# A two-layer attention and MLP kernel: row blocks transposed through DRAM in the opening, attention weights fetched from another queue

## The chip, the cores and the metric

The kernel runs on one core of a Trainium2 chip. The metric is the device time of one execution in microseconds (us), the median of the runs shown. Before the change it is 2496.91 us (three runs, 2496.49 to 2500.01).

A core has five engines that run side by side, each through its own list of instructions in order: TensorE (PE; its weight loads are PEld), VectorE (DVE), ScalarE (ACT), GpSimd (POOL) and SyncE (SP). ACT and SP also issue transfers (DMAs). An instruction that waits, for an engine or for a transfer to land, holds up all that stands behind it on its engine.

## The reference, cut to what matters

```python
def A(x, wqkv, w_phi, wo):               # S=2048, D=576, H=32, Dh=18
    q, k, v = split_heads(x @ wqkv)
    pq, pk = einsum("bhsd,hdf->bhsf", q, w_phi), einsum("bhsd,hdf->bhsf", k, w_phi)
    phi_q = concat([softmax(pq), softmax(-pq)])
    phi_k = concat([softmax(pk), softmax(-pk)])
    kv = einsum("bhsf,bhsd->bhfd", phi_k, v)
    z = einsum("bhsf->bhf", phi_k)
    num = einsum("bhqf,bhfd->bhqd", phi_q, kv)
    den = einsum("bhqf,bhf->bhq", phi_q, z)[..., None] + 1e-6
    return merge_heads(num / den) @ wo

def B(x, w1, b1, w2, b2):                # F=4608
    h = relu(x @ w1 + b1)
    return (h * h) @ w2 + b2

x = A_x
x = x + A(layernorm(x)); x = x + B(layernorm(x))
x = x + A(layernorm(x)); x = x + B(layernorm(x))
```

All is float32. There is no mask: the key totals `kv` and `z` need all 2048 rows before one query row can be finished.

## The kernel before, in words

**Precision.** A float32 operand of a matmul is kept as two parts, high and low: ACT writes the high part (rounded), DVE subtracts it from the original and gets the low part. A product is three matmuls, high x high, low x high and high x low.

**Tiling.** The 2048 rows are four blocks of 512 (`b` 0 to 3), a block four tiles of 128 rows (`t`). The opening numbers its 16 tiles straight through: `N` or `T` = 4b + t. The 576 columns are four chunks of 128 (`KC`) and a tail of 64 (`DT`). A matmul needs the normalized rows transposed, with columns on the partitions; the transposed block is a dict with `h` and `l`, the two parts.

**Stages.** The opening (0 to about 262 us) folds `w_phi` into the q and k weights, normalizes all 16 tiles, makes keys and values of every tile and adds them to the totals, and makes the queries of the last block in full, those of the others as raw rows parked in DRAM (`qs`). Behind it stands a barrier, where the totals are complete. Then come the four dense blocks of the first layer in the order 3, 2, 0, 1 (each 36 steps of 128 hidden columns, `m_3ph`, `m_2ph` and so on), with the attention of the next block and the second layer's keys and values of the previous block woven in between their steps; then a shorter second opening, `between` (1349 to 1475 us), and the four dense blocks of the second layer.

**The order of the work.** PE, ACT, DVE and POOL carry out their instructions in the order in which the program writes them. A `Plan` sets it: `plan.on(slot, depth, call, ...)` and `plan.put` put a call into a slot, and within a slot calls of a larger depth are written first (9 comes first; the projections of a slot have 0; -1 comes behind them). In the opening a slot is one half of a projection of one tile (14 matmuls). SP is not ordered by hand: a scheduler places its transfers, most of them well ahead of need.

**The line of the opening.** The list `line` gives each `T` the slots of its key projection (`k`), the value projection of the next tile (`v`) and, for `T` from 2 to 9, raw queries (`far`): six slots for each `T` in that stretch. Behind each key projection comes its soft part, on the path DVE (two maxima `s0K..m`, a difference `s0K..e`), POOL (the second difference), ACT (the exponential `s0K..e`), DVE (sums `s0K..r`, reciprocal, scaling), and later PE adds keys times values (`kvp`, `ks.add`). Also in the opening, `PrepareO` splits the output weights piece by piece into their parts (`oh` by ACT, `or` by DVE), one piece with each `T` from 4 to 8.

**Layer norm and transposes in the opening.** Class `Norm`: `stats` (DVE: BN_STATS twice, BN_AGGR; POOL: the reciprocal root), `scale_by_act` (ACT writes the normalized row, 512 columns into `n_..n` and 64 into `n_..e`), `turn` (PE transposes four 128x128 pieces into PSUM, `n_..p`; ACT writes the high part from there, DVE the low part) and `rest` (the same for the tails of two tiles at once, two transposes). All four blocks of the opening use it. In the profile its names have the block's number: `n_2n` belongs to block 2, so to the tiles `N` = 8 to 11.

**The way through DRAM.** Class `TripNorm` is there already and serves the dense blocks: the normalized row is written with its columns regrouped, stored to a scratch array in DRAM (`xrm`, the tails `xrt`) by a DMA that ACT issues, fetched back by another that ACT issues (`n`; on odd tiles also the tails of the pair, `e`), flipped in 32x32 pieces by one DVE instruction (STREAM_TRANSPOSE, `flip`), and split by ACT and DVE from SBUF. PE has no part in it. The fetch reads what the store wrote, so ACT waits at the fetch until the store has landed.

**Attention weights.** `asked(which, name)` makes tiles for one of the four weights and four calls that load it in pieces, as DMAs of SP. `plan_keys` asks for the second layer's `v` and `k` weights, once in each dense block but the first; the next block's attention asks for `o`. In the loop of `body` these calls have depth 9.

## Time and profile before

| | |
|---|---|
| median of three runs | 2496.91 us (2496.49 to 2500.01) |
| the profiled execution | 2497.19 us, its span 2495.5 us |
| PE busy | 2478.5 us, 99% of the span |
| DVE busy | 1260.1 us, 50% |
| ACT busy | 788.1 us, 32% |
| opening and barrier | 0 to 262 us |
| dense blocks of layer 0 | 262 to 1349 us |

A row of the timeline has the start in us, the duration, the engine, the line and operation, and what is written from what; in square brackets the idle time of the engine just before it and what ended that. Numbers of buffers are left out of names. `xN` counts instructions that were joined into one row. "ACTq" and "SPq" are the issue of a DMA by that engine; the transfer itself lasts beyond it. A row of the windows gives for a stretch its length, the busy time of each engine, the granted clock of PE, the share of time in which the 16 DMA engines were busy, and GB/s.

### The profile page before, as it was taken

Reading aid. Unit: us, or ns where it says so; the run is one execution under the profiler, and the core shown is the slowest. Engines: PE = TensorE matmul, PEld = TensorE weight load, DVE = VectorE, ACT = ScalarE, POOL = GpSimd, SP = SyncE. Lnnn points to the kernel's source line nnn. Section 1 sums busy time; section 2 is a strip of 40 time slices with the busy share of each in tenths; the row PEclk is TensorE's granted clock in tenths of the full one; section 3 lists DMA queues with packets and bytes.
Section 4 is the critical chain, followed back from the end, with each engine's and each line's share of the span. In section 5 each row is a group of like instructions: output and inputs, shape, how many; then the busy total and the mean of one; then the engine's idle time right before and its main releaser. Section 6 shows DMA issues by size and latency. Waiting matters only on the chain.

```text
span 2495.5 us, 37635 instructions
## 1 busy us (share of the span) xinstructions
PE 2478.5 (99%) x14968; PEld 2182.9 (87%) x14968; DVE 1260.1 (50%) x2214; ACT 788.1 (32%) x1439; POOL 189.4 (8%) x539
## 2 busy tenths in 40 slices
PE   9999999999999999999999999999999999999999
PEld 8999888888888888888888988888888888888887
DVE  6679885545744476455113776433453436442112
ACT  5444453422232223223213332413233222312212
POOL 4211100000200001000000011000110002000000
PEclk9999999999999999999999999999999999999999
DMA  9313698986767677684565248678576867676565
GB/s 321 98 54 92 243 315 266 310 315 205 259 229 271 217 206 273 216 298 146 195 199 182 92 141 263 209 217 291 186 257 204 261 219 246 217 230 230 194 199 171
DMA packets 214374, 545.07 MB, mean 218 GB/s; under 512 B 29006, under 2 KB 96814, under 8 KB 214198
## 3 DMA queue, kind: packets, MB, share of 16 engines
q1 hardware_dynamic: 163638, 500.44, 60.8%
q10 hardware_dynamic: 50560, 42.21, 5.3%
q8 instruction: 119, 1.95, 0.3%
q14 instruction: 57, 0.47, 0.1%
HBM read 439.20 MB, written 103.38 MB: 217 GB/s over the span
## 4 chain that ended last, share of the span: by engine, by line
PE 95%; DMA 2%; DVE 1%; ACT 1%; issue 1%; SPq 0%; ACTq 0%; DVEq 0%
PE m_1ph L975 9%; PE m_3ph L975 9%; PE m_0ph L975 9%; PE m_2ph L975 9%; PE m_1acc L1000 7%; PE m_3acc L1000 7%; PE m_2acc L1000 7%; PE m_0acc L1000 7%; PE m_1acc L992 2%; PE m_3acc L992 2%; PE m_2acc L992 2%; PE m_0acc L992 2%; PE a_0po L816 1%; PE a_2po L816 1%; PE kvp L593 1%; PE a_3po L816 1%
## 5 line engine op out<-in xcount | busy, mean ns | idle before, releaser
L975 PE MATMUL m_2ph<-a_2nh,m_2h 128*128 128x512 f32 x720 | 225.2, 394 | 1.2 <-ACT m_2hr L980 0.7
L975 PE MATMUL m_0ph<-a_0nh,m_0h 128*128 128x512 f32 x720 | 225.0, 394 | 1.3 <-ACT m_0hr L980 1.1
L1000 PE MATMUL m_3acc<-m_3s,m_3hb 128*128 128x448 f32 x864 | 189.3, 367 | 0.4 <-DVE m_3hb L984 0.4
L1000 PE MATMUL m_1acc<-m_1s,m_1hb 128*128 128x448 f32 x864 | 189.0, 367 | 0.3 <-PE m_1ph L975 0.3
L1000 PE MATMUL m_2acc<-m_2s,m_2hb 128*128 128x448 f32 x864 | 188.9, 367 | 0.0
L1000 PE MATMUL m_0acc<-m_0s,m_0hb 128*128 128x448 f32 x864 | 188.8, 367 | 0.0
L984 DVE CAST m_2hb<-m_2hr 128x512 fp32r<-128x512 f32 x72 | 31.2, 433 | 292.4 <-ACT m_2hr L981 292.3
L1000 PEld LDWEIGHTS m_1acc<-m_1s,m_1hb 128*128 128x128 f32 x864 | 161.9, 188 | 18.8 <-PE m_1ph L975 0.5
L1000 PEld LDWEIGHTS m_3acc<-m_3s,m_3hb 128*128 128x128 f32 x864 | 161.2, 188 | 17.8 <-PE m_3ph L975 0.6
L1000 PEld LDWEIGHTS m_2acc<-m_2s,m_2hb 128*128 128x128 f32 x864 | 161.6, 188 | 17.2
L1000 PEld LDWEIGHTS m_0acc<-m_0s,m_0hb 128*128 128x128 f32 x864 | 161.6, 188 | 17.2
L975 PEld LDWEIGHTS m_2ph<-a_2nh,m_2h 128*128 128x128 f32 x720 | 135.3, 188 | 32.7 <-ACT m_2hr L980 1.2
L975 PEld LDWEIGHTS m_0ph<-a_0nh,m_0h 128*128 128x128 f32 x720 | 135.2, 188 | 32.8 <-ACT m_0hr L980 1.5
L984 DVE CAST m_1hb<-m_1hr 128x512 fp32r<-128x512 f32 x72 | 30.7, 427 | 258.8 <-ACT m_1hr L981 258.8
L980 ACT ACTIVATE m_2hr<-m_2ph,b1t 128x512 f32<-128x512 f32 x72 | 49.6, 689 | 339.1 <-PE m_2ph L975 327.4
L980 ACT ACTIVATE m_1hr<-m_1ph,b1t 128x512 f32<-128x512 f32 x72 | 49.6, 689 | 319.1 <-PE m_1ph L975 309.1
L980 ACT ACTIVATE m_0hr<-m_0ph,b1t 128x512 f32<-128x512 f32 x72 | 49.6, 689 | 317.2 <-PE m_0ph L975 288.6
L984 DVE CAST m_0hb<-m_0hr 128x512 fp32r<-128x512 f32 x72 | 31.5, 438 | 229.0 <-ACT m_0hr L981 229.0
L984 DVE CAST m_3hb<-m_3hr 128x512 fp32r<-128x512 f32 x72 | 31.7, 440 | 173.6 <-ACT m_3hr L981 173.6
L980 ACT ACTIVATE m_3hr<-m_3ph,b1t 128x512 f32<-128x512 f32 x72 | 49.6, 689 | 219.3 <-PE m_3ph L975 209.2
L975 PE MATMUL m_3ph<-t0onh,m_3h 128*128 128x512 f32 (+1 forms) x380 | 112.9, 384 | 0.6 <-ACT t0onh L385 0.5
L975 PE MATMUL m_1ph<-t1onh,m_1h 128*128 128x512 f32 (+1 forms) x380 | 112.4, 382 | 0.8 <-ACT t1onh L385 0.5
(2050 smaller groups left out, 5734.9 us busy)
## 6 DMA issues: line engine op xcount, KB each, us to landing
m_2h<-dw SPq DMA_DIRECT2D x72, 640.0 KB
m_0h<-dw SPq DMA_DIRECT2D x72, 640.0 KB
...
```

What stands on the lines that cost most here:

```text
L593: nc.tensor.matmul(po[32 * q : 32 * q + 32, :, j], vt[:, h * VW : h * VW + 32], e[:, :, h * DH : (h + 1) * DH], start=not stay, stop=True, ...
L816: nc.tensor.matmul(pt[:, :HP], a, m[:w, g], start=(g == 0 and k == 0), stop=(g == NG - 1 and k == 2))
L975: nc.tensor.matmul(ph[:, cols], a, m, start=(k == 0), stop=(k == 3 * KC + 1))
L980: nc.scalar.activation(hr, ph, AF.Relu, bias=b1t[:, f : f + 1])
L984: nc.vector.tensor_copy(hh, hr)
L992: nc.tensor.matmul(acc[KC], a, m, start=(f == 0 and k == 0), stop=(f == NF - 1 and k == 2))
L1000: nc.tensor.matmul(acc[t][:, :R], a[:, rows], m, start=(f == 0 and k == 0), stop=(f == NF - 1 and k == 2))
```

## The change

It has two parts that do not touch one another.

In the opening, blocks 2 and 3 (tiles 8 to 15) get a `TripNorm` in place of a `Norm`: their transposes go through DRAM and DVE, tails included. `TripNorm` gets a `scale_by_act`, so that ACT and not DVE writes the row. Loads and `stats` of these tiles come one slot earlier than before, those of block 3 five slots earlier, and `scale` comes one to eight slots earlier; store, fetch and flip get slots of their own, each behind that slot's projections.

In the dense blocks of layer 0, the loads of the second layer's `v` and `k` weights and of the next blocks' `o` weights are issued by ACT, at depth -1, in place of SP at depth 9; the totals of the tiles 2 and 3 of each block are added one turn later.

```diff
--- before.py
+++ after.py
@@ -299,7 +299,7 @@
                 nc.sync.dma_start(d.rearrange("p (h c n) -> p h c n", h=2, c=NC)[:w, :, g],
                                   piece.rearrange("p (h n) -> p h n", h=2))
 
-    def asked(which, name, tags=TAGS_A):
+    def asked(which, name, tags=TAGS_A, by=nc.sync):
 
         pair, calls = [], []
 
@@ -307,7 +307,7 @@
             if k == 0:
                 pair.append(piece_tiles(f"{name}{which}{half}", tags))
             for d, piece in moved(which, half, k, pair[half][k]):
-                nc.sync.dma_start(piece, d)
+                by.dma_start(piece, d)
 
         return pair, [lambda half=half, k=k: ask(half, k) for half in range(2) for k in range(2)]
 
@@ -400,17 +400,31 @@
             super().__init__(dst, name, then)
             self.b, self.trips, self.tails, self.row = b, trips, tails, {}
 
+        def ends(self, h):
+            return self.xd.rearrange("p t e -> p (t e)")[h * DT : (h + 1) * DT]
+
+        def begin(self, t):
+            if not self.tails and self.xd is None:
+                self.xd = sb.tile([P, NT, DT], F32, tag="xd", name=f"{self.name}e", bufs=1)
+            row = self.row[t] = sb.tile([P, D], F32, tag="qk", name=f"{self.name}r{t}", bufs=5)
+            return [(row[:, : KC * P].rearrange("p (a b c) -> p b a c", a=KC, b=KC),
+                     slice(0, KC * P)), (row[:, KC * P :] if self.tails else self.xd[:, t], slice(KC * P, D))]
+
+        def scale_by_act(self, t):
+            if t not in self.trips:
+                return super().scale_by_act(t)
+            x, (nmr, rstd) = self.x.pop(t), self.stat.pop(t)
+            for dst, cols in self.begin(t):
+                src = x[:, cols] if cols.start else x[:, cols].rearrange("p (b a c) -> p b a c", a=KC, b=KC)
+                nc.scalar.activation(dst, src, AF.Identity, bias=nmr, scale=rstd)
+
         def scale(self, t):
             if t not in self.trips:
                 return super().scale(t)
             x, (mv, rstd) = self.x.pop(t), self.stat.pop(t)
-            if self.xd is None:
-                self.xd = sb.tile([P, NT, DT], F32, tag="xd", name=f"{self.name}e", bufs=1)
-            row = self.row[t] = sb.tile([P, D], F32, tag="qk", name=f"{self.name}r{t}", bufs=5)
-            args = dict(scalar1=mv[:, 0:1], scalar2=rstd, op0=ALU.subtract, op1=ALU.mult)
-            nc.vector.tensor_scalar(row[:, : KC * P].rearrange("p (a b c) -> p b a c", a=KC, b=KC),
-                                    x[:, : KC * P].rearrange("p (b a c) -> p b a c", a=KC, b=KC), **args)
-            nc.vector.tensor_scalar(row[:, KC * P :] if self.tails else self.xd[:, t], x[:, KC * P :], **args)
+            for dst, cols in self.begin(t):
+                src = x[:, cols] if cols.start else x[:, cols].rearrange("p (b a c) -> p b a c", a=KC, b=KC)
+                nc.vector.tensor_scalar(dst, src, scalar1=mv[:, 0:1], scalar2=rstd, op0=ALU.subtract, op1=ALU.mult)
             if self.then:
                 self.then(t, x)
 
@@ -422,13 +436,12 @@
                 nc.scalar.dma_start(xrt[self.b][t].rearrange("a p f -> p a f"),
                                     row[:, KC * P :].rearrange("p (a f) -> p a f", f=32))
 
-        def ends(self, h):
-            return self.xd.rearrange("p t e -> p (t e)")[h * DT : (h + 1) * DT]
-
         def fetch(self, t):
             xn = self.xn[t] = sb.tile([P, KC * P], F32, tag="xn", name=f"{self.name}n{t}")
             nc.scalar.dma_start(xn, xrm[self.b][t].rearrange("a (r g) f -> (a r) (g f)", g=KC))
             if self.tails and t % 2:
+                if self.xd is None:
+                    self.xd = sb.tile([P, NT, DT], F32, tag="xd", name=f"{self.name}e", bufs=1)
                 nc.scalar.dma_start(self.ends(t // 2).rearrange("p (t f) -> p t f", t=2),
                                     xrt[self.b][t - 1 : t + 1].rearrange("t a (r g) f -> (a r) t (g f)", g=KC))
 
@@ -1288,7 +1301,8 @@
         vpair = [piece_tiles(f"w0v{h}", TAGS_A) for h in range(2)]
         fold = Fold(kpair, vpair)
         xT = [{} for _ in range(NB)]
-        norms = [Norm(xT[b], f"n0_{b}") for b in range(NB)]
+        norms = [Norm(xT[b], f"n0_{b}") if b < 2 else TripNorm(xT[b], f"n0_{b}", b, None, range(NT), True)
+                 for b in range(NB)]
         xin = {}
 
         def load_rows(N):
@@ -1381,11 +1395,23 @@
                 plan.on(max(unit["k", added] + 8, unit["v", added] + (3 if added < 13 else 4)), 6, ks.add, T)
         for N in range(NT, NB * NT):
             at = unit["k", N - NT]
-            late = {2 * NT: 6, 2 * NT + 1: 2, 3 * NT: 6, 3 * NT + 1: 2}.get(N, 0)
-            plan.on(at - 4, 9, load_rows, N)
-            plan.on(at + 3, 2.5, stats, N)
-            plan.on(at + 4 + late // 2, 3.5, scale, N)
-            plan.on(at + 6 + late, -1, turn, N)
+            if N < 2 * NT:
+                plan.on(at - 4, 9, load_rows, N)
+                plan.on(at + 3, 2.5, stats, N)
+                plan.on(at + 4, 3.5, scale, N)
+                plan.on(at + 6, -1, turn, N)
+                continue
+            norm, t = norms[N // NT], N % NT
+            if N >= 3 * NT:
+                at -= 4
+            end = at + 11 + (4 if N == 3 * NT else 0)
+            plan.on(at - 5, 9, load_rows, N)
+            plan.on(at + 2, 2.5, stats, N)
+            plan.on(at + 3, 3.5, scale, N)
+            plan.on(at + 5, -1, norm.store, t)
+            plan.on(end - 4, -1, norm.fetch, t)
+            plan.on(end - 1, -1, norm.flip, t)
+            plan.on(end, -1, turn, N)
         o = PrepareO()
         for g in range(NG):
             at = unit["k", 4 + g]
@@ -1479,7 +1505,7 @@
                 if i + 1 < NB:
                     nb, n2 = order[i + 1], f"a{layer}_{order[i + 1]}"
                     if i or layer:
-                        o = asked("o", n2, TAGS_C)
+                        o = asked("o", n2, TAGS_C, nc.sync if layer else nc.scalar)
                     if i == 0:
                         plan_attend(plan, 1, 3, layer, nb, [other.raws[t] for t in range(NT)], nxt, n2, o,
                                     TAGS_C if layer else None)
@@ -1491,7 +1517,7 @@
                             nc.sync.dma_start(raws2[t], qs[nb][t])
 
                         for n, call in enumerate(o[1]):
-                            plan.put(at + n, 9, call)
+                            plan.put(at + n, -1, call)
                         plan_attend(plan, at - 4.5, 2, layer, nb, raws2, nxt, n2, o, TAGS_A, take, 2)
                     else:
                         raws2, held = [], {}
@@ -1518,10 +1544,11 @@
         m = f"1_{pb}"
         xk, es, ks, vts = {}, {}, {}, {}
         plan_norm(plan, Norm(xk, f"n{m}"), lambda t: done[t], (0, 0, 1, 2), (1, 1, 2, 3), (2, 3, 4, 4.5), (3, 5), (3,))
-        (vw, vcalls), (kw, kcalls) = asked("v", f"w{m}"), asked("k", f"w{m}", TAGS_C)
+        vw, vcalls = asked("v", f"w{m}", by=nc.scalar)
+        kw, kcalls = asked("k", f"w{m}", TAGS_C, nc.scalar)
         for n in range(4):
-            plan.put(8 + n if last else 2 + n / 2, 9, vcalls[n])
-            plan.put(n / 2, 9, kcalls[n])
+            plan.put(8 + n if last else 2 + n / 2, -1, vcalls[n])
+            plan.put(n / 2, -1, kcalls[n])
         if not last:
             for n in range(4):
                 plan.put(5 + n / 2, -1, lambda n=n: spill(pb, xk, [n]))
@@ -1549,7 +1576,7 @@
             plan.put(6 + t, 2, soft2, t)
             if not last:
                 plan.put(4.5 + t, 0, values, t)
-                plan.put(8.5 + t // 2 * 2, 3, add, t)
+                plan.put(8.5 + t // 2 * 3, 3, add, t)
         if last:
             keep.update(x=xk, es=es, v=vw, k=kw)
         return 11.5
```

How the instructions stand now, at three places. In a row stand the line, the operation, what is written from what, and the partitions and elements; the number behind a name tells buffers apart.

ACT in the opening, from the first half of the key projection of tile 6 (`s0k6p`) on. Before (`n_2h` is the high part of the tiles 8 and 9, `n_2n` at the end the row of tile 10):

```order
L517 ACTIVATE s0ks_1593<-s0k6p_1594 128x288
L385 ACTIVATE n_2h<-n_2p_1612 128x4x128
L517 ACTIVATE s0ks_1593<-s0k6p_1619 128x288
L296 ACTIVATE oh_1635<-or_1452 126x576
L509 ACTIVATE s07v_1712<-s07pv_1715 128x16x18
L385 ACTIVATE n_2h<-n_2p_1731 128x4x128
L394 ACTIVATE n_2h<-n_2p_1738 64x256
L553 ACTIVATE s0K6e<-s0K6e 128x1152
L509 ACTIVATE s07v_1712<-s07pv_1754 128x16x18
L343 ACTIVATE n_2n_1773<-x_10_1496,n_2b_1752,n_2d_1748 128x512
L344 ACTIVATE n_2e<-x_10_1496,n_2b_1752,n_2d_1748 128x64
```

With the change (`n_2h` is the high part of tile 8; `xrm`, `xrt` the stores of tile 9, behind them its fetches; `n_2r` the row of tile 10):

```order
L464 ACTIVATE n_2h<-n_2n_1494 128x4x4x32
L433 DMA xrm_103<-n_2r_1536 128x4x128
L436 DMA xrt_107<-n_2r_1536 128x2x32
L530 ACTIVATE s0ks_1603<-s0k6p_1604 128x288
L530 ACTIVATE s0ks_1603<-s0k6p_1622 128x288
L441 DMA n_2n_1638<-xrm_103 128x512
L445 DMA n_2e<-xrt_107 64x2x128
L296 ACTIVATE oh_1642<-or_1457 126x576
L522 ACTIVATE s07v_1727<-s07pv_1730 128x16x18
L419 ACTIVATE n_2r_1748<-x_10_1476,n_2b_1719,n_2d_1715 128x4x4x32
L419 ACTIVATE n_2r_1748<-x_10_1476,n_2b_1719,n_2d_1715 128x64
L566 ACTIVATE s0K6e<-s0K6e 128x1152
```

Stores and fetches stand between the evictions; the high part of tile 8 stands ahead of the store of tile 9, the fetch of tile 9 ahead of the next piece `oh`, and the row of tile 10 ahead of the exponential of tile 6 and no longer behind it.

DVE in the same place, from the low part of tile 8 (`n_2l`) to the sums of tile 6 (`s0K6r`). Before:

```order
L386 TENSOR_TENSOR n_2l<-n_2p_1612,n_2h 128x4x128
L297 TENSOR_TENSOR or_1452<-or_1452,oh_1635 126x576
L529 TENSOR_REDUCE s0K6m<-s0ks_1593 128x32
L530 TENSOR_REDUCE s0K6m<-s0ks_1593 128x32
L543 TENSOR_TENSOR s0K6e<-s0ks_1593,s0K6m 128x576
L386 TENSOR_TENSOR n_2l<-n_2p_1731,n_2h 128x4x128
L395 TENSOR_TENSOR n_2h<-n_2p_1738,n_2h 64x256
L349 BN_STATS n_2s_1744<-x_10_1496 128x6 x2
L358 BN_AGGR n_2m_1747<-n_2s_1744 128x2
L556 TENSOR_REDUCE s0K6r<-s0K6e 128x64
```

With the change (the STREAM_TRANSPOSE is that of tile 9 and of the tails of 8 and 9):

```order
L465 TENSOR_TENSOR n_2l<-n_2n_1494,n_2h 128x4x4x32
L297 TENSOR_TENSOR or_1457<-or_1457,oh_1642 126x576
L349 BN_STATS n_2s_1711<-x_10_1476 128x6 x2
L358 BN_AGGR n_2m_1714<-n_2s_1711 128x2
L542 TENSOR_REDUCE s0K6m<-s0ks_1603 128x32
L543 TENSOR_REDUCE s0K6m<-s0ks_1603 128x32
L556 TENSOR_TENSOR s0K6e<-s0ks_1603,s0K6m 128x576
L569 TENSOR_REDUCE s0K6r<-s0K6e 128x64
L570 RECIPROCAL s0K6r<-s0K6r 128x64
L450 STREAM_TRANSPOSE n_2n_1638<-n_2n_1638 128x512
L453 STREAM_TRANSPOSE n_2e<-n_2e 64x256
L579 TENSOR_TENSOR s0K6e<-s0K6e,s0K6r 128x1152
```

The statistics of tile 10 stand behind `or` and ahead of the maxima of tile 6, where they stood behind its difference; the flip of tile 9 follows the reciprocal of tile 6.

The `o` weights of block 0's attention in layer 0 (`a_0o`, two halves in two parts each, with rows of 126 and 72 partitions). Before, on SP, among the loads of the dense weights (`m_2h`, `m_2s`):

```order
L310 DMA a_0o0h<-kept_oh 126x1152
L1491 DMA a_0qs_6911<-qs_0_125 128x576
L1491 DMA a_0qs_7113<-qs_1_126 128x576
L1491 DMA a_0qs_7282<-qs_2_127 128x576
L310 DMA a_0o0h<-kept_oh 72x288
L310 DMA a_0o0l<-kept_ol 126x1152
L938 DMA m_2h_10_6999<-dw_10_151 128x1280
L310 DMA a_0o0l<-kept_ol 72x288
L1491 DMA a_0qs_7404<-qs_3_128 128x576
L310 DMA a_0o1h<-kept_oh 126x1152
L950 DMA m_2s_9_6986<-dw_9_186 128x1152
L310 DMA a_0o1h<-kept_oh 72x288
```

With the change, on ACT, among the dense step's two instructions (`m_2hr`) and the exponentials of the attention:

```order
L310 DMA a_0o0h<-kept_oh 126x1152
L310 DMA a_0o0h<-kept_oh 72x288
L566 ACTIVATE a_0Q1e<-a_0Q1e 128x1152
L993 ACTIVATE m_2hr_7368<-m_2ph_7353,b1t 128x512
L994 ACTIVATE m_2hr_7368<-m_2hr_7368 128x512
L310 DMA a_0o0l<-kept_ol 126x1152
L310 DMA a_0o0l<-kept_ol 72x288
L745 DMA phs_0_109<-a_0z_7313 128x4x160
L745 DMA phs_0_109<-a_0z_7320 128x4x160
L993 ACTIVATE m_2hr_7425<-m_2ph_7410,b1t 128x512
L994 ACTIVATE m_2hr_7425<-m_2hr_7425 128x512
L310 DMA a_0o1h<-kept_oh 126x1152
```

Each piece now stands behind the two instructions of a dense step, and ahead of what ACT does next for the attention, an exponential or the stores into `phs` and the fetch from there.

## The prediction

> **What bounds the kernel now.** I read the page first, then PE's waits, then the windows of the opening, and last the timelines and the tiles of the operations that the change touches.
>
> ```profile
> PE 2478.5 (99%) x14968; PEld 2182.9 (87%) x14968; DVE 1260.1 (50%) x2214; ACT 788.1 (32%) x1439; POOL 189.4 (8%) x539
> ```
>
> PE is busy for 99% of the span. So the kernel can gain only where PE instructions go away or where PE waits, and it loses as soon as another engine falls behind PE's pace. PE's waits from 600 to 1100 us, where most of the second part of the change lies:
>
> ```profile
> PE kv_3k L593 <- issue: 1.2, 1, 1.2
> PE m_0ph L975 <- ACT m_0hr L980: 1.1, 1, 1.1
> PE m_2ph L975 <- ACT m_2hr L980: 0.7, 1, 0.7
> PE m_2ph L975 <- DMA m_2h<-dw: 0.5, 1, 0.5
> ```
>
> They sum to 3.5 us, the most that the second part can give. The first part works in the opening, where the stretch ahead of the barrier reads:
>
> ```profile
> 157.00:232.00 75.00, 74.89 (x918) 73.24 (x917) 67.19 (x91) 31.93 (x62) 6.05 (x17) 1.00 0.19 53
> ```
>
> Of 75 us PE works 74.89, and DVE 67.19 of them: the shares of the whole span hide that DVE is almost full here.
>
> **What the first part removes.** The transposes of tiles 8 to 15. One tile, on PE:
>
> ```profile
> 99.71 0.60 PE L384 MATMUL n_2p<-ident,n_2n 128*128 128x128 f32 x4
> 100.06 0.38 PE L493 MATMUL s0k6p<-w0k1h,n_1h 128*128 128x288 f32 x1
> ```
>
> The next projection begins 0.35 us later. The two tail transposes of a pair add about half of that, 0.18 (an estimate by the same row). That makes 8 x 0.35 + 4 x 0.18 = 3.5 us off PE, if nothing else holds PE up.
>
> **What it adds, and the loop it closes.** The durations are those of the same operations in the dense blocks:
>
> ```profile
> L437 DVE STREAM_TRANSPOSE a_0nn<-a_0nn x8: 657/704/725, 780.3 to 1715.3; 128x512 f32<-128x512 f32 x8
> L451 ACT ACTIVATE a_0nh<-a_0nn x8: 1103/1126/1139, 786.3 to 1716.0; 128x512 fp32r<-128x512 f32 x8
> L452 DVE TENSOR_TENSOR a_0nl<-a_0nn,a_0nh x8: 1081/1090/1114, 787.5 to 1717.2; 128x512 fp32r<-128x512 f32 x8
> ```
> ```profile
> L440 DVE STREAM_TRANSPOSE a_0ne<-a_0ne x4: 394/420/443, 790.6 to 1716.0; 64x256 f32<-64x256 f32 x4
> L462 ACT ACTIVATE a_0nh<-a_0ne x4: 657/662/677, 793.6 to 1717.2; 64x256 fp32r<-64x256 f32 x4
> L463 DVE TENSOR_TENSOR a_0nh<-a_0ne,a_0nh x4: 611/614/618, 795.0 to 1718.3; 64x256 fp32r<-64x256 f32 x4
> ```
>
> The present pass of one tile on DVE, that of key tile 7, shows the rest, with the low parts from PSUM (`L386`, `L395`) that go away; behind it ACT's rows:
>
> ```profile
> 116.95 0.76 DVE L297 TENSOR_TENSOR or<-or,oh 126x576 fp32r<-126x576 f32 x1 [1.55 <-ACT oh L296]
> 117.62 0.75 DVE L529 TENSOR_REDUCE s0K7m<-s0ks 128x32 f32<-128x576 f32 x1
> ...
> 119.61 0.81 DVE L349 BATCH_NORM_STATS2 n_2s<-x 128x6 f32<-128x288 f32 x2
> 120.46 0.21 DVE L358 BATCH_NORM_AGGREGATE n_2m<-n_2s 128x2 f32<-128x12 f32 x1
> 121.96 1.35 DVE L556 TENSOR_REDUCE s0K7r<-s0K7e 128x64 f32<-128x1152 f32 x1 [1.29 <-ACT s0K7e L553]
> 123.35 0.55 DVE L557 RECIPROCAL s0K7r<-s0K7r 128x64 f32<-128x64 f32 x1
> ...
> 126.27 0.69 DVE L386 TENSOR_TENSOR n_2l<-n_2p,n_2h 128x512 fp32r<-128x512 f32 x1 [0.97 <-ACT n_2h L385]
> 126.99 0.42 DVE L395 TENSOR_TENSOR n_2h<-n_2p,n_2h 64x256 fp32r<-64x256 f32 x1
> ```
> ```profile
> 116.24 0.68 ACT L296 ACTIVATE oh<-or 126x576 fp32r<-126x576 f32 x1
> ...
> 122.21 0.82 ACT L343 ACTIVATE n_2n<-x,n_2b,n_2d 128x512 f32<-128x512 f32 x1
> 122.94 0.43 ACT L344 ACTIVATE n_2e<-x,n_2b,n_2d 128x64 f32<-128x64 f32 x1
> ```
>
> Today nothing of one tile's norm holds up the next tile's softmax. In the order after the change it does. Follow the two lists: on ACT the store of tile 9 stands behind the high part of tile 8, which needs the flip of tile 8; the fetch of tile 9 holds ACT until that store has landed; behind the fetch stands `oh`; on DVE `or` needs `oh`, and behind `or` stand the statistics of tile 10, the maxima, differences and sums of key tile 6, and only then the flip of tile 9. That flip releases the store of tile 10. It is a closed loop, one pass for each tile, and each link is a wait in order on one engine.
>
> How long a store of 256 KB takes to land in the opening no row shows. Near it are these:
>
> ```profile
> 74.09 0.35 SPq L1366 DMA_DIRECT2D qs<-f0qs  x1
> 79.03 0.95 SPq L299 DMA_DIRECT2D kept_oh<-oh  x1
> 80.08 0.85 SPq L299 DMA_DIRECT2D kept_ol<-or  x1
> 83.83 0.35 SPq L1279 DMA_DIRECT2D x<-in_A_x  x1
> ```
> ```profile
> DMA  7898773005999999720000000000000000000000
> ```
> ```profile
> SPq L1279 <- DMA kept_ol<-or: 14.2, 4, 4.4
> ```
>
> The load of `x` waits for `kept_ol`, 283.5 KB, issued 3.75 us earlier and with `kept_oh` right ahead of it: an upper end. The second fence is the DMA activity from 74 to 78 us: the store `qs`, 288 KB, issued at 74.09 and alone, moves its last packets at 75.8, 1.7 us later; with its signal I take 1.8 as the lower end. I take 2.6, just below the middle, since the opening's engines are mostly idle (share 0.19 in the window above) but these packets are four times as many. The Trainium skill, page "DMA: Bandwidth & Descriptors", section "Anatomy of one DMA", fits 2.0 us plus the bytes at 436 GB/s for GpSimd's path, with most of the fixed part spent on the receipt of the write; for 256 KB that is an estimate of 2.6 us. The 1.7 to 3.75 us of the rows hold that value.
>
> One pass: flip 0.70, high part 1.13, landing 2.6, issue of the fetch 0.34 (its row stands further below), `oh` 0.68, `or` 0.76, statistics 0.81 + 0.21, from the first maximum to the sums 121.96 - 117.62 = 4.34, sums and reciprocal 1.35 + 0.55. That is 13.5 us; on every second tile 0.66 for the tails' high part: 13.8 us on average. The pace today, from the sums of tile 5 to those of tile 9:
>
> ```profile
> L556 DVE TENSOR_REDUCE s0K5r<-s0K5e x1: 1354/1354/1354, 96.7 to 96.7; 128x64 f32<-128x1152 f32 x1
> ...
> L556 DVE TENSOR_REDUCE s0K9r<-s0K9e x1: 1354/1354/1354, 145.1 to 145.1; 128x64 f32<-128x1152 f32 x1
> ```
>
> (145.1 - 96.7) / 4 = 12.1 us. So each pass loses 1.7 us. From the flip of tile 8 to that of tile 11 there are three passes: 5.1 us. Before the flips of tiles 10 and 11 there now also stand the statistics of tiles 12 and 13, 1.02 us of DVE each, and ahead of the high parts their rows, 0.82 + 0.43 us of ACT. On each engine that is 1.0 to 1.3 us, and the two follow one another, since the row needs the statistics: some 2 us a pass, 4 in all. PE meets this where it takes up the value projection of tile 10: about 9 us late. The 3.5 us of transposes don't come off this, as PE is then waiting.
>
> From there to the barrier DVE sets the pace. Tiles 12 to 15 add 0.70 + 1.09 each and take 0.69 away, and the two tail pairs add 0.42 + 0.61 - 0.42: 4 x 1.10 + 2 x 0.61 = 5.6 us, against 75 - 67.19 = 7.8 us of gaps, most of which are waits for exponentials that the flips don't fill in this order (DVE also sits out the 1.13 us of ACT between flip and low part). I take 7, with 0 and 8 as ends. The barrier cannot absorb it, as PE waits there for DVE's last product. Opening: 9 + 7 = +16 us.
>
> **The second part.** The waits on ACT, 1.1 and 0.7 us, come from this:
>
> ```profile
> 789.04 0.37 ACTq L419 DMA_DIRECT2D xrm<-a_0nr  x1
> ...
> 799.77 0.34 ACTq L430 DMA_DIRECT2D a_0nn<-xrm  x1
> ```
>
> The fetch sat for the store, 10.7 us, while SP's loads of dense weights and of `k` weights were on their way. The `k` weights now come later, as do the `o` weights that delayed a load of `m_2h` (0.5): 2.3 us can come back, and 1.2 more for `kv_3k`, whose totals move a turn later. Against it, ACT now issues eight loads for each weight pair, some ahead of a fetch, each held by an earlier transfer on its lane: nothing to 3 us in two blocks. I take -2.5 us in all, with -3.5 and +1 as ends.
>
> **Sum.** 16 - 2.5 = +13.5 on the profiled 2497.2 us, which is 0.3 above the median of the runs: 2511 us. With a landing of 1.8 the three passes lose 2.4 less, with no loss on DVE behind them 7 less: 2501. With 3.75 they lose 3.5 more, the barrier 1 more and the second part 3.5 more: 2519.
>
> **Rivals.**
> *The loop stays hidden.* PE's 3.5 us come off and the whole dense gain of 3.5: 2497.2 - 7.0 = 2490 us. For it speaks that ACT is idle more than half of this stretch. But a pass must then take 12.1 us or less, so the store must land within 2.6 - 1.7 = 0.9 us: half of the lower end. Chance 0.11.
> *Only DVE's extra work counts.* The passes are absorbed by slack, 5.6 us of DVE reach the barrier, the dense blocks give 2.5: 2500 us, no change that can be told. Chance 0.10.
> *ACT blocks in the dense blocks.* A weight load of ACT waits for an earlier transfer as that fetch did, 10.7 us, and each such stall costs PE what the two in the rows did, about 0.9. With five of them, in addition to the opening and without the gain: 16 + 4.5 = 2518. Chance 0.11.
> *PE's clock falls in its gaps.* The window of the opening shows clock 1.00 (the column behind POOL), and PE's waits above reach 1.2 us, so no run here shows what a gap of several us does. If the clock halved after the gap ahead of tile 10 for one half projection (a sixth of the pass of 12.1 us), PE would lose 2 us; after two gaps 4: 2515. Chance 0.05. The Trainium skill states such a rule on the page "TensorE: Matmul & The Clock Gate", section "Why this matters for your kernels": no idle gap of PE above about 3 us, or the clock is halved.
>
> **How the numbers follow.** The forecast has 0.63. A change under 0.2% (5 us) can't be told from none here. Slower: 0.63 + 0.11 + 0.05 = 0.79; the same: 0.10; faster: 0.11. The range from 2499 to 2519 us holds the forecast with its ends, both slower rivals and the second rival's own time; it leaves out the faster case and part of the same.
>
> **What would show it.** Right: in the changed profile ACT idle before `oh` or the `n_2n` fetch, released by the store of `xrm`; sums `s0K5r` to `s0K9r` some 14 us apart; PE waiting several us at `s010pv` for `n_2h`; the barrier about 16 us late. Right for the second part: no wait on `m_2hr` at 800 us and none at 1090. Wrong: sums still 12.1 us apart, or a barrier at 225 us, which would be the hidden loop; new waits on `m_2h`, `m_0h` or `kv` in the dense blocks would be the ACT rival; a granted clock below 1.00 from 140 to 160 us the last.

## The result and the profile after

The changed kernel takes 2532.58 us (median of 4 executions, 2526.14 to 2533.82) against 2497.12 us for the kernel before, timed on the same chip. The ratio is 1.0135, with a 95% interval from 1.0121 to 1.0149: slower by 35.5 us. The forecast was 2511 us, with a range up to 2519. The sign was right; the size was not. The profiled execution took 2533.82 us; the head of its page:

```profile
span 2532.1 us, 37616 instructions
PE 2484.4 (98%) x14928; PEld 2183.0 (86%) x14928; DVE 1269.8 (50%) x2226; ACT 790.2 (31%) x1439; POOL 192.0 (8%) x539
PEclk9989999999999999999999999999999999999999
```

PE has 40 instructions fewer (the 32 transposes of blocks and the 8 of tails), DVE 12 more, and the clock row has one 8, in the third slice of 63 us. PE's busy time is 5.9 us longer than before, with fewer instructions, and its idle time grew from 17.0 us of the span (2495.5 - 2478.5) to 47.7 (2532.1 - 2484.4): most of the loss is waiting. PE's waits of the whole program show where:

```profile
PE s010pv L506 <- DVE n_2h L476: 7.7, 1, 7.7
PE m_2acc L1013 <- DVE m_2hb L997: 4.6, 3, 3.0
PE m_0acc L1013 <- DVE m_0hb L997: 4.5, 3, 2.9
PE m_0ph L988 <- DMA m_0h<-dw: 2.8, 1, 2.8
PE kvp L606 <- DVE s0K11e L579: 2.5, 1, 2.5
```

(The columns are the sum in us, the number of waits, and the longest.) The first row is the forecast's wait at the value projection of tile 10. The two behind it lie in the dense blocks 2 and 0, where the prediction put a gain. The size of each loss is read from landmarks, the start of the same group of matmuls before and after. Three of them, from the groups of matmuls by line and shape, before:

```profile
L793 PE MATMUL t0opn<-t0of,kbh x40: 278/339/387, 230.9 to 252.0; 126*126 126x256 f32 x32, 72*72 72x256 f32 x8
L493 PE MATMUL k_2kp<-w_2k0h,n_2h x20: 288/293/378, 842.1 to 885.7; 128*128 128x288 f32 x20
L493 PE MATMUL k_0kp<-w_0k0h,n_0h x20: 288/294/378, 1132.1 to 1164.7; 128*128 128x288 f32 x20
```

and after:

```profile
L806 PE MATMUL t0opn<-t0of,kbh x40: 277/339/386, 248.6 to 269.6; 126*126 126x256 f32 x32, 72*72 72x256 f32 x8
L506 PE MATMUL k_2kp<-w_2k0h,n_2h x20: 288/292/378, 871.6 to 915.3; 128*128 128x288 f32 x20
L506 PE MATMUL k_0kp<-w_0k0h,n_0h x20: 288/295/378, 1168.8 to 1201.5; 128*128 128x288 f32 x20
```

So PE is 17.7 us late behind the barrier, 29.5 us late at the second layer's key projection of block 2, which stands in dense block 0, and 36.7 us late at that of block 0, which stands in dense block 1. With more such pairs of the same matmul, in order of time:

| place (PE) | late by, us | added there |
|---|---|---|
| value projection of tile 10 (`s010pv`), where PE goes on behind its wait | 8.4 | 8.4 |
| 5 us later | 10.5 | 2.1 |
| last projections before the barrier | 16.7 | 6.2 |
| first dense block | 18.6 | 1.9 |
| dense block 2, ahead of the first wait beside its `o` loads | 17.6 | -1.0 |
| dense block 2, behind them | 26.1 | 8.5 |
| dense block 0, key projection of block 2 | 29.5 | 3.4 |
| dense block 0, behind its `o` loads | 37.5 | 8.0 |
| dense block 1, key projection of block 0 | 36.7 | -0.8 |

The opening costs 18.6 us where 16 were forecast. The dense blocks cost another 18 where a gain of 2.5 was forecast, most of it in two steps of about 8 us that stand beside the `o` weights' loads.

### The profile page after: what moved, and what is told of

It is laid out like the page before. It is cut to its first block, busy times and chain, and to the rows that moved or that the text cites. A ratio compares the mean times of both kernels' runs of the same rounds, so it can differ in the third digit from the quotient of the medians.

```text
span 2532.1 us, 37616 instructions
## 1 busy us (share of the span) xinstructions
PE 2484.4 (98%) x14928; PEld 2183.0 (86%) x14928; DVE 1269.8 (50%) x2226; ACT 790.2 (31%) x1439; POOL 192.0 (8%) x539
## 4 chain that ended last, share of the span: by engine, by line
PE 88%; DVE 4%; DMA 4%; ACT 2%; POOL 1%; issue 1%; ACTq 0%; SPq 0%; DVEq 0%; POOLq 0%
PE m_1ph L988 9%; PE m_3ph L988 9%; PE m_0ph L988 9%; PE m_2ph L988 8%; PE m_3acc L1013 7%; PE m_1acc L1013 7%; PE m_0acc L1013 6%; PE m_2acc L1013 6%; PE m_1acc L1005 2%; PE m_3acc L1005 2%; PE m_0acc L1005 2%; PE m_2acc L1005 2%; PE a_0po L829 1%; PE a_2po L829 1%; PE a_3po L829 1%
## 5 line engine op out<-in xcount | busy, mean ns | idle before, releaser
L1013 PEld LDWEIGHTS m_3acc<-m_3s,m_3hb 128*128 128x128 f32 x864 | 161.3, 188 | 17.7 <-PE m_3ph L988 0.5
L988 PE MATMUL m_0ph<-a_0nl,m_0h 128*128 128x512 f32 x288 | 113.6, 394 | 0.0
```

The source lines that it names most:

```text
L988: nc.tensor.matmul(ph[:, cols], a, m, start=(k == 0), stop=(k == 3 * KC + 1))
L1013: nc.tensor.matmul(acc[t][:, :R], a[:, rows], m, start=(f == 0 and k == 0), stop=(f == NF - 1 and k == 2))
```

## The experiments

The times are medians; "+" is the difference to the kernel before, timed again beside it.

**The two parts alone.** First the opening alone: the weights stay on SP, the totals at their old turn. Then the weights and totals alone: all blocks keep `Norm`.

```diff
 # e1_opening
-o = asked("o", n2, TAGS_C, nc.sync if layer else nc.scalar)
+o = asked("o", n2, TAGS_C)
-plan.put(at + n, -1, call)
+plan.put(at + n, 9, call)
 # v and k weights likewise; the totals:
-plan.put(8.5 + t // 2 * 3, 3, add, t)
+plan.put(8.5 + t // 2 * 2, 3, add, t)
 # e2_weights: of the changed kernel; the tiles 8 to 15 also get back their slots of before
-norms = [Norm(xT[b], f"n0_{b}") if b < 2 else TripNorm(...) for b in range(NB)]
+norms = [Norm(xT[b], f"n0_{b}") for b in range(NB)]
```

> The opening's part alone; weights on SP and the totals' slots as before the change. The two parts act in places that do not overlap, so theory A (each part costs by itself) expects what the trace of the change shows up to the first dense block, +18.5 us: about 2515.5 us, with PE waiting 7 to 8 us at s010pv and no wait of ACT on o weights at 660 to 690 us. Rival B (the dense blocks lose only because the late opening shifts them against SP's loads) expects the whole +35 us here: about 2532 us.

> The weights' part alone (v, k and o weights issued by ACT in the dense blocks of layer 0, totals of tiles 2 and 3 a turn later), the opening as before. Theory A expects what the blocks 2 and 0 lost in the trace of the change, +17.5 us: about 2514.5 us, with ACT waiting 5 to 13 us on o weights and on phs stores in each of the two blocks. Rival B expects the gain that the prediction put there, 2 to 3 us: about 2494 us.

The opening alone: 2516.31 us, +19.0, ratio 1.0081 [1.0063, 1.0099]. The second part alone: 2508.16 us, +10.9, ratio 1.0048 [1.0032, 1.0065]. Both lose. The second part, which the prediction counted as a gain, is about a third of the loss by its own run, and 16.5 of the 35.5 us if the opening's 19.0 are taken off. The two runs together give 29.9 us; the 5.6 us between were not traced to a cause, and the second part's own executions spread from 2504.1 to 2518.1 us.

**Which loads.** The `o` weights alone on ACT, and the `v` and `k` weights alone on ACT, each with everything else as before:

```diff
 # e5_o_alone: of the kernel before
-o = asked("o", n2, TAGS_C)
+o = asked("o", n2, TAGS_C, nc.sync if layer else nc.scalar)
-plan.put(at + n, 9, call)
+plan.put(at + n, -1, call)
 # e6_kv_alone: of the kernel before
-(vw, vcalls), (kw, kcalls) = asked("v", f"w{m}"), asked("k", f"w{m}", TAGS_C)
+vw, vcalls = asked("v", f"w{m}", by=nc.scalar)
+kw, kcalls = asked("k", f"w{m}", TAGS_C, nc.scalar)
 # ... and their depth 9 -> -1
```

> Only the o weights are issued by ACT (depth -1); v and k weights by SP, totals and opening as before. Theory A1 (the o loads stand on ACT in the middle of the attention's store and fetch of phs, and every one waits for an earlier transfer on its lane) expects 8 us for each of two blocks: about 2513 us. Rival A2 (the bunched v and k loads, 5.9 MB in some 25 us, are what costs) expects less than 3 us: 2497 to 2500 us.

> Only the v and k weights of the second layer's keys are issued by ACT (depth -1); o weights by SP, totals and opening as before. Theory A1 expects the 1.2 and 4.6 us that the trace of the change lost at the first steps of blocks 2 and 0, less some 1.6 us that the k weights give back at the xrm stores of both blocks: about 2501 us. Rival A2 expects most of the loss of the dense blocks here: 2509 to 2513 us.

The `o` loads alone: 2511.40 us, +14.1, ratio 1.0053 [1.0037, 1.0069]. The `v` and `k` loads alone: 2495.99 us, -1.3, ratio 0.9999 [0.9989, 1.0008], no difference. The latter bring new waits, PE's from 520 to 1100 us:

```profile
PE m_0ph L988 <- DMA m_0h<-dw: 2.2, 1, 2.2
PE m_2ph L988 <- DMA m_2h<-dw: 2.2, 1, 2.2
```

but the waits on `m_0hr` and `m_2hr` of 1.1 and 0.7 us are gone, and nothing of it reaches the end. The profiled execution with the `o` loads alone was the fastest of its five, 2504.70 us, and so shows only about half of their median loss. What the `o` loads do stands in ACT's order of work. In the changed kernel (start, duration, and in brackets the wait ahead; ACTq is a transfer that ACT issues):

```profile
674.19 0.78 ACTq L310 DMA_DIRECT2D a_0o1l<-kept_ol  x2
675.56 1.89 ACTq L745 DMA_DIRECT2D phs<-a_0z  x2
677.83 0.69 ACT L993 ACTIVATE m_2hr<-m_2ph,b1t 128x512 f32<-128x512 f32 x1 [3.01 <-PE m_2ph L988]
678.55 0.63 ACT L994 ACTIVATE m_2hr<-m_2hr 128x512 f32<-128x512 f32 x1
691.61 0.34 ACTq L752 DMA_DIRECT2D a_0e<-phs  x1
692.00 1.16 ACT L566 ACTIVATE a_0Q3e<-a_0Q3e 128x1152 f32<-128x1152 f32 x1 [12.82 <-DMA phs<-a_0z]
```

and at the same place before:

```profile
654.34 0.93 ACTq L732 DMA_DIRECT2D phs<-a_0z  x2
659.93 0.69 ACT L980 ACTIVATE m_2hr<-m_2ph,b1t 128x512 f32<-128x512 f32 x1 [5.02 <-DVE a_0Q2e L566]
660.65 0.63 ACT L981 ACTIVATE m_2hr<-m_2hr 128x512 f32<-128x512 f32 x1
660.79 0.34 ACTq L739 DMA_DIRECT2D a_0e<-phs  x1
```

Attention stores the query features of a tile (`phs`, two stores of 320 KB, as much together as one piece of the `o` weights, 648 KB) and fetches them back turned (`a_0e`), both issued by ACT. Before, the fetch goes out 6.4 us after the store. Now a piece of the `o` weights stands just ahead of the store in ACT's order, and the fetch goes out 16.0 us after it. ACT stands idle for 12.8 us around the fetch, and what is behind it, the exponential of attention and the ReLU of the next dense step, is late: PE waits 1.6 us for that ReLU. The fetch of the tile ahead was late too, 12.0 us after its store (659.97 and 672.01 us), and DVE, which flips what it brings, waits for it with the attention's work and the high part of a ReLU (`m_2hb`) behind that flip:

```profile
681.28 1.51 DVE L762 STREAM_TRANSPOSE a_0e<-a_0e 128x1280 f32<-128x1280 f32 x1 [2.06 <-DMA a_0e<-phs]
687.73 0.73 DVE L997 CAST m_2hb<-m_2hr 128x512 fp32r<-128x512 f32 x1
```

Before, that flip starts at 656.01 us without a wait. PE waits for the high part and then for the ReLU (PE's timeline in the changed kernel):

```profile
688.51 3.02 PE L1013 MATMUL m_2acc<-m_2s,m_2hb 128*128 128x448 f32 x12 [2.99 <-DVE m_2hb L997]
691.37 0.86 PE L1005 MATMUL m_2acc<-m_2hb,m_2s 128*128 128x512 f32 x3
693.80 0.49 PE L988 MATMUL m_2ph<-a_2nh,m_2h 128*128 128x512 f32 x1 [1.56 <-ACT m_2hr L993]
```

With the `o` loads alone the same rows read 654.13 for the store and 667.46 for the fetch, 13.3 us. The move shifted the loads in time as well: SP had issued those of this block from 594.8 to 610.9 us, ahead of the first `phs` store at 641.6; ACT issues them from 651.3 to 675.0, with the stores from 660.0 on among them. If the loads among the stores are the cause, the same loads issued by the same engine some turns earlier, where no `phs` store is near, should cost nothing. The counter-test leaves them on SP in the otherwise changed kernel, and a third run moves only the totals:

```diff
 # e10_o_early: of e5_o_alone
-plan.put(at + n, -1, call)
+plan.put(8 + n, -1, call)      # at is 11.5: 3.5 turns earlier
 # e3_o_on_sp: of the changed kernel
-o = asked("o", n2, TAGS_C, nc.sync if layer else nc.scalar)
+o = asked("o", n2, TAGS_C)     # and depth 9
 # e4_add_later: of the kernel before
-plan.put(8.5 + t // 2 * 2, 3, add, t)
+plan.put(8.5 + t // 2 * 3, 3, add, t)
```

> As the run with only the o weights on ACT, but their four pieces stand 3.5 turns earlier, ahead of the attention's stores and fetches of phs and no longer among them. Theory O expects the loss of 14 us to go: 2496 to 2499 us, with no wait of ACT on phs above 3 us. Rival W (any wide load on ACT holds it up by the waits on its lane and delays the dense step behind) expects the loss to stay, 2508 to 2514 us, only at an earlier place.

> The whole change, but with the o weights on SP as before (v and k weights on ACT, totals a turn later, opening through DRAM). Theory O (the o loads, put into ACT's queue between store and fetch of phs, are the whole loss of the dense blocks) expects the opening's 19 us and nothing else: 2515 to 2517 us. Rival K (with the opening late, the bunched v and k loads cost the 6 us that the trace of the change shows in its first steps of blocks 2 and 0) expects 2520 to 2522 us.

> Only the totals of the tiles 2 and 3 of the second layer's keys are added a turn later; all else as before the change. Both theories on the weights expect the stall of 1.2 us at kv_3k and its like in block 0 to go: -1 to -2.5 us, 2494.5 to 2496 us. If the stall only moves, 2497 us.

The `o` loads on ACT, but earlier: 2495.70 us, -1.8, ratio 0.9991 [0.9982, 1.0000]. The loss is gone, and ACT, whose `o` loads now go out from 604.4 to 626.5 us, reads

```profile
652.76 0.93 ACTq L745 DMA_DIRECT2D phs<-a_0z  x2
658.35 0.69 ACT L993 ACTIVATE m_2hr<-m_2ph,b1t 128x512 f32<-128x512 f32 x1 [5.02 <-PE m_2ph L988]
659.08 0.63 ACT L994 ACTIVATE m_2hr<-m_2hr 128x512 f32<-128x512 f32 x1
659.16 0.34 ACTq L752 DMA_DIRECT2D a_0e<-phs  x1
```

6.4 us again. The whole change with `o` on SP: 2518.41 us, +20.9, ratio 1.0085 [1.0070, 1.0100]; so the `o` loads are worth 35.5 - 20.9 = 14.6 us in the changed kernel, as much as alone. The totals alone: 2497.16 us, +0.5, ratio 0.9998 [0.9989, 1.0008]: the wait on `kv_3k` (1.2) goes, and one of 1.4 us, `m_2acc` on DVE's `a_0nl`, comes. Shown is that these loads, issued by ACT among the `phs` stores, cost 14 us by the medians (10.9 in the run of the second part alone), and that 3.5 turns earlier they cost nothing. Not shown is whether the order in ACT's queue does it or the time of the transfers: SP never issued them at the later time. The transfers of the changed kernel speak for both. From the store at 675.6 us to the end of its fetch's wait, the queue that carries it (q10) moves 1.97 MB, where it moves 0.66 MB, the store alone, at the same place before; but in the last 4 us, 687 to 691, it moves only 0.16 MB, in 260 packets of the store's size, beside 0.86 MB of SP's loads.

**Breaking the loop of the opening.** The sums of tiles 5 to 9 in the changed kernel, first and last of five rows:

```profile
L569 DVE TENSOR_REDUCE s0K5r<-s0K5e x1: 1353/1353/1353, 97.5 to 97.5; 128x64 f32<-128x1152 f32 x1
...
L569 DVE TENSOR_REDUCE s0K9r<-s0K9e x1: 1354/1354/1354, 154.4 to 154.4; 128x64 f32<-128x1152 f32 x1
```

(154.4 - 97.5) / 4 = 14.2 us a pass. The single passes are 14.1, 12.4, 16.5 and 13.9 us. The forecast was 13.8, and about 2 more in the last two, where statistics and rows of block 3 stand ahead: 14.8 on average. The first pass on ACT:

```profile
100.04 1.14 ACT L464 ACTIVATE n_2h<-n_2n 128x512 fp32r<-128x512 f32 x1 [1.68 <-DVE n_2n L450]
100.05 0.37 ACTq L433 DMA_DIRECT2D xrm<-n_2r  x1
100.51 0.47 ACTq L436 DMA_DIRECT2D xrt<-n_2r  x1
101.02 0.91 ACT L530 ACTIVATE s0ks<-s0k6p 128x288 f32<-128x288 f32 x2
102.76 0.34 ACTq L441 DMA_DIRECT2D n_2n<-xrm  x1
104.29 0.65 ACTq L445 DMA_DIRECT2D n_2e<-xrt  x1
104.98 0.69 ACT L296 ACTIVATE oh<-or 126x576 fp32r<-126x576 f32 x1 [3.05 <-DMA xrt<-n_2r]
```

The order is the one that the prediction followed: high part, store, fetch 2.7 us behind the store, `oh` behind the fetch. From store to fetch it is 2.7, 2.4 and 3.6 us at three tiles in a row, where 2.6 was taken. Two terms of its sum were off, in opposite ways. The store is issued as the high part starts, 100.05 against 100.04 us, so the 1.13 us of the high part are no link of this pass. And the tails' pair was left out: `xrt` takes 3.8 us from store to fetch, and `oh` waits for that one, 2.2 us behind the first fetch, where 0.34 was taken. Two kernels take `oh` out of the loop, one by putting it ahead of the fetch, one by giving the fetches to SP; two more split the part by blocks; a last one gives block 3 the slots of block 2, so that all its steps come four slots later (of tile 12 only loads, statistics, row and store):

```diff
 # e7_oh_first: of e1_opening
-plan.on(at + 1, -1, o.split, g)
+plan.on(at + 1, -0.5, o.split, g)
 # e8_sp_fetch: of e1_opening, for the opening's TripNorms
-nc.scalar.dma_start(xn, xrm[self.b][t]...)
+nc.sync.dma_start(xn, xrm[self.b][t]...)       # tails likewise
 # e9_block2 / e12_block3: of e1_opening
-... TripNorm(...) for blocks 2 and 3
+... TripNorm(...) for block 2 alone / block 3 alone, the other as before the change
 # e11_later3: of e8_sp_fetch
-if N >= 3 * NT:
-    at -= 4
-end = at + 11 + (4 if N == 3 * NT else 0)
+end = at + 11
```

> The opening's part alone (as in the run of the opening alone), and in it one order changed: the split of the next o piece (oh) stands ahead of the fetch on ACT, not behind it. Theory L (the loop through the blocking fetch sets the pace) expects the pass to lose landing and issue of the fetch, 2.6 + 0.34 us, to about 11 us, below PE's 12.1 us: no PE wait above 2 us up to s010pv, an opening that is late by DVE's extra work only, 4 to 8 us, so 2501 to 2505 us. Rival M (statistics ahead of the maxima, high parts and rows on ACT set the pace) expects little change: 2512 to 2516 us.

> The opening's part alone, with the fetches of the opening issued by SP in place of ACT (stores stay on ACT). No store holds up ACT any more. Theory L expects the same as from the changed order or a little better, 2500 to 2505 us: passes of 12.1 us up to tile 8, then what DVE's extra 5.6 us leave at the barrier. Rival M expects 2512 to 2516 us. If SP's own transfers wait behind a fetch for its store, x loads would come late and the statistics with them.

> The opening's part alone and for block 2 only (tiles 8 to 11 through DRAM, tiles 12 to 15 on PE with the slots of before). Theory L expects three passes of 13.8 us in place of 12.1 and no statistics of block 3 among them: PE 4 to 6 us late at s010pv, DVE's 3 us of added work in a stretch that still has gaps, so +4 to +7: 2501 to 2504 us. Rival (DVE at the barrier sets the loss, the loop is only its slack) expects +0 to 2, less 1.8 us of transposes: 2495 to 2499 us.

> The opening's part alone and for block 3 only (tiles 12 to 15 through DRAM in the slots of the change, tiles 8 to 11 on PE with the slots of before; fetches on ACT). If the two blocks' losses add up, as theory S has it, the 19 us less the 2 of block 2 alone: 2512 to 2515 us. If the loop of tiles 8 to 11 is needed for the loss, 2502 to 2506 us, the 5.6 us of DVE work and little else.

> The opening's part alone with the fetches on SP, and the tiles 12 to 15 in the slots that tiles 8 to 11 have, four slots later than in the change (loads, statistics, row, store, fetch, flip and turn). Theory S (half of what is left of the loss, some 6 us, comes from the statistics and rows of block 3 that were brought ahead of the flips of tiles 10 and 11) expects PE at s010pv no later than 2 us and 2503 to 2506 us. Rival D (DVE's added work near the barrier is the whole rest, wherever it stands) expects 2509 to 2512 us.

| kernel | us | to before | ratio, 95% interval |
|---|---|---|---|
| e1, whole opening | 2516.31 | +19.0 | 1.0081 [1.0063, 1.0099] |
| e7, `oh` ahead of the fetch | 2511.26 | +14.6 | 1.0049 [1.0034, 1.0064] |
| e8, fetches on SP | 2509.76 | +13.1 | 1.0044 [1.0029, 1.0059] |
| e11, and block 3 later | 2502.03 | +4.5 | 1.0020 [1.0011, 1.0030] |
| e9, block 2 alone | 2499.34 | +2.7 | 1.0006 [0.9996, 1.0016] |
| e12, block 3 alone | 2506.34 | +8.8 | 1.0039 [1.0025, 1.0054] |

Taking `oh` away from the fetch gains 4.4 to 5.9 us by the medians, so the loop is real, but it is less than half of the loss; the 2500 to 2505 us expected of a loop that is all of it did not come. The pass of tile 7 to 8 shows what is left, with the fetches on SP:

```profile
L569 DVE TENSOR_REDUCE s0K7r<-s0K7e x1: 1353/1353/1353, 121.4 to 121.4; 128x64 f32<-128x1152 f32 x1
L569 DVE TENSOR_REDUCE s0K8r<-s0K8e x1: 1352/1352/1352, 135.7 to 135.7; 128x64 f32<-128x1152 f32 x1
```

14.3 us, and with block 3 later as well:

```profile
L569 DVE TENSOR_REDUCE s0K7r<-s0K7e x1: 1353/1353/1353, 121.4 to 121.4; 128x64 f32<-128x1152 f32 x1
L569 DVE TENSOR_REDUCE s0K8r<-s0K8e x1: 1352/1352/1352, 132.5 to 132.5; 128x64 f32<-128x1152 f32 x1
```

11.1 us. Moving block 3 is worth another 8.6 us, the largest single term. In the changed kernel DVE takes the statistics of tile 12 ahead of the flip of tile 10 (125.81 and 126.73 us), and ACT waits 4.28 us to write the row of tile 12 (128.80) ahead of the high part of tile 10 (130.14). The run moves loads, stores and flips along with them, so which of these steps counts is not shown. That block 3's steps hold up block 2 would also explain why the blocks don't add up, 2.7 (not to be told from nothing) and 8.8 alone, 19.0 together; no run separates it. What remains in e11, 4.5 us, stands beside waits of PE that now lie further on (2.5 us on `s0K13e`, 1.7 on `n_3h`).

**The clock behind the gap.** The rival with PE's clock is there to be seen. Windows of the changed kernel (from:to, length, the engines' busy time from PE to POOL, granted clock, DMA share, GB/s):

```profile
145.00:148.00 3.00, 0.00 (x0) 0.00 (x0) 0.78 (x1) 2.14 (x4) 0.83 (x1) 0.50 0.23 66
150.00:152.00 2.00, 1.90 (x8) 1.90 (x9) 1.97 (x4) 0.42 (x1) 0.36 (x1) 0.50 0.46 160
156.00:158.00 2.00, 2.00 (x17) 2.00 (x17) 1.97 (x6) 0.41 (x1) 0.56 (x2) 1.00 0.27 91
```

and PE's timeline at the end of the gap:

```profile
150.10 0.61 PE L506 MATMUL s010pv<-w0v0h,n_2h 128*128 128x288 f32 x1 [7.67 <-DVE n_2h L476]
150.50 0.44 PE L506 MATMUL s010pv<-w0v0l,n_2h 128*128 128x288 f32 x1
```

The clock falls to 0.50 within the gap and is back only 4.5 us after PE has started again; at 0.50 there are 8 matmuls in 2 us, at 1.00 there are 17. The 4.5 us hold some 18 matmuls at 0.24 us in place of 0.13: 2 us. The Trainium skill, page "TensorE: Matmul & The Clock Gate", section "Why this matters for your kernels", states the rule: no idle gap of PE above about 3 us, or the clock is halved. The gap of 7.7 us agrees with it. Around 3 us this execution has no sharp limit: the clock also falls behind waits of 2.5, 2.8 and 2.9 us (which end at 185.2, 863.2 and 989.3 us), and does not behind one of 3.0 us (1.00 from 688.5 to 692):

```profile
185.40:188.80 3.40, 3.40 (x70) 3.32 (x57) 3.33 (x6) 1.09 (x2) 0.18 (x2) 0.50 0.00 0
864.60:868.00 3.40, 3.40 (x10) 2.66 (x9) 0.00 (x0) 0.00 (x0) 0.00 (x0) 0.50 1.03 409
990.90:994.30 3.40, 3.40 (x10) 2.62 (x9) 0.18 (x1) 1.38 (x2) 0.00 (x0) 0.50 0.24 49
```

Whether the 2 us behind the first gap reach the end was tried by filling it with 72 transposes of the identity, whose result nobody reads:

```diff
 # e13_filled_gap: of e1_opening
+def fill():
+    pad = wtile("fill")
+    for i in range(72):
+        nc.tensor.transpose(pad[:, i % NT * P : (i % NT + 1) * P], ident, ident)
+plan.on(unit["v", 10], 0.5, fill)
```

> The opening's part alone (2516 us) with 72 transposes of the identity put into PE's gap ahead of s010pv, whose result nobody reads; they take some 6.3 of the 7.9 us of that gap. In the run without them PE's granted clock falls to 0.5 in the gap and matmuls stand 0.24 us apart in place of 0.13 for some 4.5 us after it, about 2 us. Theory: the clock stays at 1.0 here, but PE waits for DVE again at the totals of tiles 11, 12 and 14, so those 2 us do not reach the end: 2515 to 2517 us, with 2 us more of PE waits there. Rival: the clock's loss adds to the end: 2514 us or less.

In the filled gap the clock stays at 1.00:

```profile
152.00:154.00 2.00, 2.00 (x17) 2.00 (x17) 1.81 (x3) 0.41 (x1) 0.70 (x1) 1.00 0.11 41
```

yet the time is 2518.70 us, +21.5, ratio 1.0079 [1.0065, 1.0093], not better than e1. PE's next wait grew instead:

```profile
PE kvp L606 <- DVE s0K11e L579: 4.5, 1, 4.5
```

from 2.7 us without the filling. The trial is not a clean one: the filling takes 8.0 us where 6.3 were expected, PE goes on behind its wait at 151.8 us in place of 150.4, and so only 0.5 us of the 2 are left when it reaches the next wait, for DVE's product, which comes later itself. DVE sets the pace there: a PE that is ahead waits longer. The times alone could hide 2 us, but the start of `t0opn` behind the barrier, 250.2 us against 248.9 without the filling, shows no gain either. The second fall, behind the wait on `s0K11e`, was not filled; with that wait at 4.5 us it lasts longer here, 0.50 from 185 to 191 us. So no run shows a cost of the first fall at the end, and the part of the second is open. In dense block 0 PE's lag grew by 1.6 and 1.9 us in the two stretches at 0.50 shown above and did not shrink again in that block; no run tried those.

**What is worth keeping.** Block 2 alone with its fetches on SP, without and with the early `o` loads, and the early `o` loads with the `v` and `k` loads:

```diff
 # e16_block2_sp_only: of e9_block2
-nc.scalar.dma_start(xn, xrm[self.b][t]...)
+nc.sync.dma_start(xn, xrm[self.b][t]...)       # tails likewise
 # e14_block2_sp, e17_again: of e16
+plan.put(8 + n, -1, call)      # o weights on ACT, as in e10
 # e15_early_and_kv: of e10_o_early
+vw, vcalls = asked("v", f"w{m}", by=nc.scalar)  # k likewise, depth -1
```

> Block 2 alone through DRAM in the opening, its fetches on SP, tiles 12 to 15 on PE; o weights on ACT 3.5 turns earlier; all else as before the change. The stalls of the run with block 2 alone (1.7 us at s08pv, 1.0 at s010pv) should go with ACT's wait on the stores, PE saves four tiles' transposes, 1.8 us, in a stretch where DVE still has gaps, and the early o loads give 1.5: 2493 to 2495 us. Rival: DVE paces the stretch up to the barrier anyway, so that the transposes give nothing there: 2495 to 2498 us.

> The opening as before; o weights on ACT 3.5 turns earlier and v and k weights on ACT. Each alone measured 1.0 to 1.8 us under before, inside the uncertainty. If SP's missing weight loads are what gives that (its dense loads come earlier, the xrm stores land sooner), both together 2494 to 2495.5 us; if the two loads now meet in ACT's queue, 2497 us or more.

> Block 2 alone through DRAM with its fetches on SP, and nothing else: o weights on SP at their old place. The executions of the run with both fell into two groups, 2493 to 2497 us at clock 1.000 and 2499 to 2502 us at 0.999. If the opening makes the second group (a gap of PE long enough that its clock falls), it shows here too: part of the executions near 2495, part near 2502 us. If the early o loads make it, all stand near 2495 us.

> The same kernel as in the run with block 2 on SP and early o weights, for a second profile: seven of its eleven executions were some 7 us slower than the one that was profiled. If this profile falls on such a one, its waits of PE show where the 7 us are: at the barrier or ahead of it if the opening makes them, in blocks 2 and 0 if the loads do.

e16: 2495.09 us, -2.0, ratio 0.9990 [0.9980, 1.0000]. e15: 2495.57 us, -1.7, 0.9996 [0.9987, 1.0004]. e14: 2500.60 us, ratio 1.0006 [0.9997, 1.0015]; e17, the same kernel again: 2496.37 us, -0.7, 0.9993 [0.9982, 1.0004]. The eleven executions of e14 lie in two groups, four from 2492.8 to 2497.0 and seven from 2499.5 to 2502.4; the repetition did not show the second, and its cause is open. The 2493 to 2495 us expected of e14 did not come. e16 has the lowest median of all, but 0.1% is within what can't be told from no change. At the barrier it is ahead: `t0opn` starts at 229.4 us, 1.5 before the 230.9 of the kernel before. In the profiles of e14 and e17, with the same opening, it starts at 228.8 and 229.0, and in six others whose opening is that of before at 230.2 to 232.0. That is near the 1.75 us that half of the prediction's 3.5 us of transposes would be, so that gain is there up to the barrier, once the fetches are off ACT and block 3 is left on PE.

## Why the prediction was right or wrong

**Opening, +16: right within 3 us, in part by luck.** It measured +18.6 in the trace and +19.0 alone. The loop that the prediction drew is there, and PE goes on at `s010pv` 8.4 us late, against 9, with 2.1 more behind it at half clock. But errors in the sum cancel. In the pass, the high part was counted though the store does not wait for it to end, and the tails' own store and fetch were left out; 14.2 us on average stand against 14.8. In the split, the loop through ACT, put at 5.1 us, is worth 4.4 to 5.9 (e7, e8), as priced; block 3's early steps, put at 4, are worth 8.6 (e11); and what is left, put at 7, is 4.5.

**PE's transposes: in line with the forecast.** That they give nothing while PE waits fits the runs, and in e16 one block of them gives some 1.5 us at the barrier.

**Second part, -2.5: wrong, and this is the step that failed.** The prediction said of ACT's loads: "nothing to 3 us in two blocks". They cost 14.6 us (35.5 less the 20.9 of e3), all of it by the `o` loads (e5) at that place (e10). The step asked only for how long ACT is held at the issue of a load. It did not list, as it had done in the opening, what stands behind the loads on ACT and in its transfers: the `phs` store, whose fetch holds ACT in order (16.0 us from store to fetch, against 6.4) and whose data DVE waits for. It also did not ask what else is under way when the loads go out, some 60 us later than SP had issued them (some 18 of them the late opening). The gains that it hoped for did appear as waits removed (`m_0hr`, `m_2hr`, `kv_3k`), but new waits (`m_0h`, `m_2h`, `m_2acc`) took their place, and they came to -1.3 (e6) and +0.5 (e4), neither distinguishable from nothing.

**Sum.** 19.0 + 14.6 = 33.6 of the 35.5 us; the remaining 1.9 us is what `v`, `k` and totals cost in the changed kernel (e3 less e1), within the uncertainty of both. The range ended at 2519 because its end for the second part was +1.

**Rivals.** The hidden loop and the DVE-only case are out, by the passes of 14.2 us and the times of e1. The ACT rival, 2518, named the right engine, but as the stalled instruction a weight load and not the fetch of `phs` behind it, and its price was taken from a stall of 10.7 us behind which PE waited only 0.9. Here the ReLU behind the fetch and DVE's high part behind the flip are late, and PE loses about 8 us in each of two blocks. The clock rival happened as a mechanism, with 2 us on PE behind tile 10 as worked out. There no run shows a cost at the end (e13); in dense block 0, which the rival did not name, the lag grew by 1.6 and 1.9 us at half clock.
